# A paced list of transfers: turned weights ahead of loads and outputs, and a read-back of two transfers in place of four

## The chip, the core and the metric

The kernel runs on one core of a Trainium2 chip. The metric is the device time of one execution in microseconds, and lower is better. The kernel before took 1454.44 us, the median of three runs (1446.7 to 1459.63).

## What is computed

The reference has two parts: an attention with a threshold, and a bilinear feed-forward layer over its output. All numbers are 32-bit floats.

```python
# q, k, v: 8 batches x 8 heads x 576 rows x 64;  tau = 0.02
scores = scale * np.matmul(q, k.transpose(0, 1, 3, 2))
thresh = np.max(scores, axis=-1, keepdims=True) - tau
scores = np.where(scores >= thresh, scores, -1000000000.0)
scores = scores - np.max(scores, axis=-1, keepdims=True)
attn = np.exp(scores)
attn = attn / (np.sum(attn, axis=-1, keepdims=True) + 1e-09)
x = np.matmul(attn, v)      # then (B,H,S,D) -> (B*S, H*D): 4608 x 512
out = ((x @ w_a) * (x @ w_b)) @ w_out      # w_a, w_b: 512 x 1536;  w_out: 1536 x 512
```

## The kernel before

**Attention.** Two heads of a batch make a pair; there are 32 pairs. A pair has four units of 128 rows (u = 0 to 3) and one of the last 64 rows (u = 4). The outer loop (L974) takes one unit per slot. In slot g, PE makes the scores of unit g (`scores`, L379), DVE takes their maxima (L386), ACT the exponentials (L407), DVE masks and sums them (L410), and ACT divides by the sum (L429). The result `tw` lies with rows on the partitions, while the product with v needs it turned, with keys on the partitions.

**How the weights are turned.** For the first units PE turns them. From then on it is done in three steps that follow each other through the slots:

- slot g, `turn_blocks` of unit g-1: DVE turns blocks of 32 x 32 in place (L473), and four transfers of 144 KB (72 KB for u = 4) put them into DRAM (`swap<-tw`).
- slot g, `turn_back` of unit g-2: the unit is read back from DRAM into a tile `wT`, in transfers of 144 KB (`wT<-swap`), four for a unit of 128 rows, two for the last unit of a pair. There are two `wT` buffers (L441), and a product needs both.
- slot g, `weighted` of unit g-3: where that unit is the last of a half (u = 1 or u = 4), PE makes the product `pv` of the turned weights and v (L513), from which `xT`, the input of the feed-forward layer, is copied.

**Feed-forward.** Its matmuls (L673, L746, L803) are a generator, `ffn`, of which `advance` takes so many columns between the steps of the attention. The matmuls of both parts stand on PE in the order in which the program writes them; `keep_order` fixes that order on every engine, SP's queue included.

**The list of transfers.** All transfers of the main loop are issued by SP, in order. Up to slot 40 they are issued where they are posted (L142). From slot 41 on, `post` puts each entry, with its key and slot, at the end of a list, `bulk`. `passed` takes one entry off the front for every 320 columns (`PUMP`) of PE's work. `pump` issues its transfers and makes the first one wait for the last matmul written so far (L151 and the lines after it), so that transfers are spread along PE's work. `flush` takes entries off until those of a key are out: it is called where the program is about to use the data, in `prep` (Q and K), in `turn_back` (the stores of that unit) and in `weighted` (v and the read-backs). At the start of a slot, entries that were posted before the slot ahead of it are put out too (L977).

What is posted: `("tw", i, u)`, four entries of one transfer, in `turn_blocks`; `("wT", i, h)`, four entries of one transfer (two for u = 4), in `turn_back`; in `load`, `("k", i)`, four entries of one transfer, and `("q0", i)` and `("q1", i)`, two entries of two; `("v", i)`, two entries of two; `"out"`, one entry for each tile of results (`store`). Q and K are loaded three and four slots ahead of their first scores, and DVE turns them (`prep`, L347) one and two slots ahead of them.

Each transfer takes one of eight semaphores in turn, and SP waits for the transfer eight places earlier to have landed before it issues the next with the same semaphore.

Of the kernel before, what the change touches and what calls it, by code (L numbers as in the profile page):

```python
# [53 lines left out]
def kernel(  # L54
# [81 lines left out]
    bulk = []  # L136

    def post(key, *moves):

        if not state["paced"]:  # L140
            for move in moves:
                nc.sync.dma_start(*move)  # L142
        else:
            bulk.append((key, state["slot"], moves))

    def pump(count=1):

        for _ in range(min(count, len(bulk))):
            behind = next(x.name for x in reversed(nc.cur_bb.bb.instructions) if x.engine == mybir.EngineType.PE)
            for n, move in enumerate(bulk.pop(0)[2]):  # L150
                moved = nc.sync.dma_start(*move)  # L151
                if n == 0:
                    tc.add_manual_dep(
                        moved.ins, behind,
                        mybir.DependencyInfo(mybir.DependencyClass.Sync, mybir.DependencyReason.DATA),
                        reason="pace")

    def flush(*keys):

        while any(key in keys for key, _, _ in bulk):  # L160
            pump()

    def passed(columns):

        running["pump"] = running["pump"] + columns if bulk else 0
        while running["pump"] >= PUMP:
            running["pump"] -= PUMP
            pump()

    def load(i, name):  # L170

        b, hp = pairs[i]
        src = {"q": q, "k": k}[name[0]]
        n0, n1 = {"k": (0, NB), "q0": (0, HALF // Q), "q1": (HALF // Q, NB)}[name]
        bufs = HP if name == "k" else Q_BUFS
        most = NB if name == "k" else NB - HALF // Q
        t = work.tile([P, most, Q], FP32, tag=name[0] + "T", bufs=bufs, name=name[0] + "T")[:, 0:n1 - n0]
        for j in range(2):
            rows = src[b, 2 * hp + j].rearrange("(e n) d -> e n d" if name == "k" else "(n e) d -> e n d", e=Q)
            moves = [(t[(2 * j + h) * Q:(2 * j + h + 1) * Q], rows[:, n0:n1, h * Q:(h + 1) * Q]) for h in range(2)]  # L180
            for some in ([moves] if name != "k" else [moves[0:1], moves[1:2]]):
                post((name, i), *some)
        loaded.setdefault(i, {})[name] = t
# [9 lines left out]
    def load_v(i, again=False):  # L193
        b, hp = pairs[i]
        if not again:
            loaded[i]["v"] = loads.tile([P, NSLOT, D], FP32, tag="vm", bufs=HP, name="vm")
        for j in range(2):
            rows, half = v[b, 2 * hp + j], loaded[i]["v"][j * D:(j + 1) * D]
            if i >= HP or again:
                if i < HP:  # L200
                    rows = rows.rearrange("(c s p) d -> p c s d", c=2, p=Q)
                else:
                    rows = rows.rearrange("(p c s) d -> p c s d", c=2, p=Q)
                post(("v", i), *((half[c * Q:(c + 1) * Q], rows[:, c]) for c in range(2)))
            else:
                nc.sync.dma_start(half, rows.rearrange("(s p) d -> p s d", p=D))
# [21 lines left out]
    for F in range(NF):  # L228
# [3 lines left out]
    state = {"loaded": 0, "added": 0, "converted": 0, "rows": 0, "sums": False, "through": 0, "over": False,  # L232
             "layer": False, "paced": False, "slot": 0, "reading": False, "first": 0}
# [104 lines left out]
    prepared, scored, weights, turned, whole = {}, {}, {}, {}, {}  # L338
# [4 lines left out]
    def prep(i, name):  # L343

        flush((name, i))
        mT = loaded[i].pop(name).rearrange("p n e -> p (n e)")
        nc.vector.transpose(mT, mT)  # L347
        prepared.setdefault(i, {})[name] = mT
# [91 lines left out]
    def turned_tile():  # L440
        return work.tile([P, G + 1, NSLOT, Q], FP32, tag="wT", bufs=2, name="wT")  # L441
# [17 lines left out]
    def part(i, u):  # L459

        if i < HP:
            return {1: (i, 0), 3: (i, 1), NT: (i, 2)}.get(u)
        return {1: (i, 0), NT: (i, 1)}.get(u)
# [4 lines left out]
    def turn_blocks(i, u):  # L468

        ws, _ = weights.pop((i, u))  # L470
        t = whole.pop((i, u))
        for w in ws:
            nc.vector.transpose(w, w)  # L473
        if u < NT:
            swap = scratch.tile([G, P, NSLOT * Q], FP32, tag="swap", name="swap")
        else:
            swap = scratch.tile([2, P, NSLOT * Q], FP32, tag="swapt", name="swap")
        swaps[i, u] = swap
        for g in range(G):
            if u < NT:  # L480
                to, n = swap[g], G
            else:
                to, n = swap[g % 2, (1 - g // 2) * D:(2 - g // 2) * D], 2
            post(("tw", i, u), (to.rearrange("(r p) e -> p r e", p=Q),
                                t[g * Q:(g + 1) * Q, 0:n * NSLOT].rearrange("p (r s) e -> p r (s e)", r=n)))

    def turn_back(i, u):

        flush(("tw", i, u))
        swap = swaps.pop((i, u)).rearrange("g p e -> p g e")  # L490
        key = "wT", i, min(u // 2, 1) if i >= HP else u // 2
        if u < NT or i < HP:
            turned[i, u] = turned_tile()
            n = G if u < NT else 2
            for y in range(0, n, 1):
                post(key, (turned[i, u][:, y:y + 1].rearrange("p g s e -> p g (s e)"), swap[:, y:y + 1]))
        else:
            for y in range(2):
                post(key, (turned[i, 2 + y][:, G].rearrange("p s e -> p (s e)"), swap[:, y]))
# [76 lines left out]
    def weighted(i, h):  # L576

        b, hp = pairs[i]
        flush(("v", i), ("wT", i, h))
        n = width(i, h)  # L580
        if h < 2:
            groups = G + (n > HALF)
            wT = [turned.pop((i, 2 * h + y))[:, 0:groups] for y in range(2)]
        else:
            t = turned.pop((i, NT))
            wT = [t[:, y:y + 1] for y in range(2)]
        pv = product([lambda rows, s, t=t: t[rows, :, s] for t in wT], loaded[i]["v"], n)
        read = [], []
        if h < 2:
            if hp == 0:  # L590
                x_of[b, h] = x_tile("xT")
            settle(x_of[b, h][:, hp, :], pv, 0, P, read)
            settled[b, h] = hp + 1
            if hp == HP - 1:
                del settled[b, h]
                complete.append((x_of.pop((b, h)), ("half", b, h)))
        if n % HALF:
            t = b % GT
            if hp == 0 and t == 0:
                xtail_of[b // GT] = x_tile("xt")  # L600
            settle(xtail_of[b // GT][:, hp, t * TAIL:(t + 1) * TAIL], pv, (n - TAIL) // 2, n // 2, read)
            del loaded[i], prepared[i]
            if hp == HP - 1 and t == GT - 1:
                complete.append((xtail_of.pop(b // GT), ("tail", b - t, 0)))
# [364 lines left out]
    n = 0  # L969
# [4 lines left out]
    for g in range(len(units) + PV_LAG):  # L974
        written = len(pending)
        state["slot"], state["paced"] = g, g > 40
        while bulk and bulk[0][1] < g - 1:  # L977
            pump()
# [4 lines left out]
        if BY_PE + 1 < g <= len(units) + 1:  # L983
            n = g - PV_LAG
            back = (1 if BY_PE <= n and part(*units[n]) else 0,)
            if not back[0]:
                turn_back(*units[g - 2])
        if here:
            i, u = units[g]
# [40 lines left out]
        if g > BY_PE:  # L1030
            n = g - PV_LAG
            held = 0.0
            if BY_PE <= n < len(units) and part(*units[n]):
                held = 384 - (PORTIONS[2] + PORTIONS[3]) * pace + NSLOT * width(*part(*units[n])) // 2
                held = min(max(held, 0.0), 384)
            advance(PORTIONS[1] * pace - held)
            if BY_PE <= n < len(units) and part(*units[n]):
                p, h = part(*units[n])
                if pairs[p][1] == 0:
                    make_x(2 if h == 1 and p >= HP and pairs[p][0] % GT == 0 else 1)  # L1040
                make_room()
                weighted(*part(*units[n]))
                passed(NSLOT * width(*part(*units[n])) // 2)
                running["owed"] -= NSLOT * width(*part(*units[n])) // 2
            if back and back[0] > 0:
                turn_back(*units[g - 2])
# [85 lines left out]
```

## Time and profile before

| What | Value |
|---|---|
| Median of three runs | 1454.44 us (1446.7 to 1459.63) |
| The profiled execution | 1455.69 us, its span 1453.8 us |
| TensorE clock granted, mean of the span | 0.991 |
| Transfers that SP issues | 1736, of which `wT<-swap` 544 and `swap<-tw` 608 |
| Bytes moved | 223.32 MB, 154 GB/s over the span |
| `wT<-swap`: issue, and from issue to landing (medians) | 383 ns (paced), 3.1 us |
| `swap<-tw`: from issue to landing (median, 144 KB) | 2.9 us |

The page gives busy time by engine, then the span in 40 slices, the DMA queues, the chain of work that ended last, the groups of instructions with the idle time of their engine ahead of them, and the DMA issues. PE is TensorE's matmuls, PEld its weight loads; each matmul of 32-bit floats stands as two records. SPq is SP's own queue: its instructions only issue transfers. In a row of groups the part after the bar is busy time, mean duration in ns, and the idle time of the engine just before, with what ended most of it. A row of waits reads: who waited, for whom, us in total, times, the longest. A row of stretches reads: from:to, length, then busy us and instructions of PE, PEld, DVE, ACT and POOL, the granted clock, the share of the DMA engines, GB/s. A row of the timeline reads: start, us, engine, line, operation, how many merged.

### The profile page before, as it was taken

The numbers are of one execution on the slowest core, as the hardware profiler recorded it, in microseconds if no ns is written. First come the engines' busy times: TensorE is split into PE (matmuls) and PEld (weight loads), VectorE is DVE, ScalarE is ACT, GpSimd is POOL, SyncE is SP. The second block draws the span as 40 slices with busy tenths as digits, with TensorE's granted clock in tenths as the row PEclk, the third lists the DMA queues.
The fourth block names the chain that finished last, engine by engine and source line by source line (L and its number), as shares of the span: only waits on it lengthen the run. The fifth ranks groups of instructions, "written<-read, shape, count | busy, mean of one in ns | idle before, by whom it ended". The sixth has DMA issues, their size and how long they took to land.

```text
span 1453.8 us, 77671 instructions
## 1 busy us (share of the span) xinstructions
PE 1388.9 (96%) x34208; PEld 1255.0 (86%) x34208; DVE 1017.0 (70%) x2244; ACT 684.2 (47%) x1244; POOL 480.6 (33%) x668
## 2 busy tenths in 40 slices
PE   6889999998999989999999999999999999999998
PEld 4777897987979889999999899898888879998896
DVE  6898677787767867677757686778757677755223
ACT  5787454544545445545444445344535445430110
POOL 2664803423060605132333333241506060605000
PEclk8899999999999999999999999999999999999999
DMA  9976667666756776567545676466655676450000
GB/s 203 240 217 184 157 168 200 178 162 171 190 154 152 170 188 158 151 161 191 158 121 140 159 187 191 120 158 160 190 148 138 161 184 195 122 152 28 4 18 17
DMA packets 330914, 223.32 MB, mean 154 GB/s; under 512 B 175441, under 2 KB 314705, under 8 KB 330577
## 3 DMA queue, kind: packets, MB, share of 16 engines
q1 hardware_dynamic: 328064, 217.76, 58.7%
q8 instruction: 270, 4.42, 1.3%
q10 hardware_dynamic: 2512, 0.59, 0.2%
q14 instruction: 68, 0.55, 0.1%
HBM read 128.58 MB, written 89.65 MB: 150 GB/s over the span
## 4 chain that ended last, share of the span: by engine, by line
PE 86%; DMA 5%; DVE 3%; issue 2%; SPq 2%; ACT 1%; DVEq 0%; ACTq 0%
PE pab L673 26%; PE po L803 20%; PE pab L746 18%; PE pv L513 10%; PE sc L379 10%; DMA wT<-swap 3%; PE po L849 1%; SPq L142 1%; DMA vm<-in_v_dram 1%; DMA sums_u<-in_q_dram 1%; PE tp L454 1%; DVE mx L386 1%; DVE tw L473 1%; DVE tw L410 1%; DMA sums_u<-in_k_dram 0%
## 5 line engine op out<-in xcount | busy, mean ns | idle before, releaser
L386 DVE TENSOR_REDUCE mx<-sc 128x1 f32<-128x576 f32 x288 | 206.2, 752 | 138.0 <-PE sc L379 126.7
L429 ACT ACTIVATE tw<-tw,rcp 128x576 f32<-128x576 f32 x272 | 197.8, 769 | 220.6 <-DVE rcp L423 220.6
L407 ACT ACTIVATE tw<-sc,bias,scalars 128x576 f32<-128x576 f32 x288 | 239.3, 831 | 10.1 <-ACT bias L406 0.4
L639 POOL TENSOR_TENSOR h<-h,u 128x512 f32<-128x512 f32 x28 | 35.1, 1273 | 613.8 <-DVE h L716 469.4
L803 PE MATMUL po<-wo_sb,h 64*64 64x256 f32 x3264 | 230.2, 377 | 0.0
L410 DVE SCALAR_TENSOR_TENSOR tw<-sc,thr,tw 128x576 f32<-128x576 f32 x288 | 222.9, 798 | 9.0 <-ACT tw L407 7.2
L513 PE MATMUL pv<-wT,vm 64*64 64x160 f32 (+3 forms) x5184 | 188.3, 278 | 25.7 <-DMA wT<-swap 19.3
L513 PEld LDWEIGHTS pv<-wT,vm 64*64 64x64 f32 x5184 | 169.7, 136 | 40.2 <-issue 15.1
L379 PE MATMUL sc<-kT,qT 64*64 64x288 f32 x2016 | 196.9, 404 | 3.2 <-issue 2.0
L473 DVE STREAM_TRANSPOSE tw<-tw 128x576 f32<-128x576 f32 x272 | 196.1, 754 | 0.8 <-ACT tw L429 0.8
L803 PEld LDWEIGHTS po<-wo_sb,h 64*64 64x64 f32 x3264 | 168.0, 133 | 26.7
L803 PE MATMUL po<-sums_u,h 64*64 64x256 f32 x2448 | 169.3, 376 | 0.3 <-DVE h L754 0.3
L772 POOL TENSOR_TENSOR h<-h 128x256 f32<-128x256 f32 x168 | 117.4, 730 | 124.4 <-PE po L803 120.7
L379 PEld LDWEIGHTS sc<-kT,qT 64*64 64x64 f32 x2016 | 117.9, 133 | 28.5 <-issue 5.7
L803 PEld LDWEIGHTS po<-sums_u,h 64*64 64x64 f32 x2448 | 123.0, 133 | 21.6 <-DVE h L754 1.2
L673 PE MATMUL pab<-xU,wb_sb 64*64 64x128 f32 x4096 | 137.1, 270 | 0.0
L673 PEld LDWEIGHTS pab<-xU,wb_sb 64*64 64x64 f32 x4096 | 130.0, 133 | 2.0
L406 ACT ACTIVATE bias<-mx,scalars 128x1 f32<-128x1 f32 x288 | 83.2, 289 | 88.7 <-DVE mx L386 88.5
L521 DVE COPY xT<-pv 64x128 f32<-64x128 f32 (+1 forms) x136 | 38.2, 281 | 120.1 <-PE pv L513 118.9
L520 ACT COPY xT<-pv 128x128 f32<-128x128 f32 (+1 forms) x68 | 17.6, 259 | 215.5 <-PE pv L513 215.3
L673 PE MATMUL pab<-xS,wa_sb 64*64 64x128 f32 x2048 | 112.2, 269 | 0.0
L746 PE MATMUL pab<-xS,wb_sb 64*64 64x256 f32 (+1 forms) x1536 | 101.3, 359 | 0.9 <-issue 0.9
(138 smaller groups left out, 2473.3 us busy)
## 6 DMA issues: line engine op xcount, KB each, us to landing
wT<-swap SPq DMA_DIRECT2D x544, 144.0 KB, 3.1
swap<-tw SPq DMA_DIRECT2D x480, 144.0 KB, 2.9
vm<-in_v_dram SPq DMA_DIRECT2D x128, 72.0 KB, 2.4
swap<-tw SPq DMA_DIRECT2D x128, 72.0 KB, 3.0
kT<-in_k_dram SPq DMA_DIRECT2D x112, 72.0 KB, 3.1
out_dram<-kept SPq DMA_DIRECT2D x30, 256.0 KB, 3.0
qT<-in_q_dram SPq DMA_DIRECT2D x112, 40.0 KB, 2.3
qT<-in_q_dram SPq DMA_DIRECT2D x112, 32.0 KB, 2.8
```

The source lines that it names most:

```text
L379: nc.tensor.matmul(sc[j if u < NT else 0][to, c], qT[r, q0:q0 + D], kT[r, c * SH:(c + 1) * SH], start=True, stop=True)
L386: nc.vector.tensor_reduce(mx[:, c], sc[j], axis=AX.XY, op=ALU.max)
L406: nc.scalar.activation(bias[:, j:j + 1], mx[:, j:j + 1], AF.Copy, scale=e_nscale)
L407: nc.scalar.activation(wb[j], sb[j], AF.Exp, bias=bias[:, j:j + 1], scale=e_scale)
L410: nc.vector.scalar_tensor_tensor(out=wv, in0=sb[j], scalar=thr[:, j:j + 1], in1=wv, op0=ALU.is_ge, op1=ALU.mult, accum_out=sums[:, j:j + 1])
L429: nc.scalar.activation(w, w, AF.Copy, scale=rcp[:, j:j + 1])
L473: nc.vector.transpose(w, w)
L513: nc.tensor.matmul(pv[c * D:(c + 1) * D, y], vm[rows, s], wT[y](rows, s), start=(s == 0), stop=(s == NSLOT - 1))
L673: nc.tensor.matmul(out[c * D:(c + 1) * D, r, f * P:(f + 1) * P], w[g][k][rows, w0:w0 + D], moving[k][rows], start=(fresh and k == 0 and f ...
L746: nc.tensor.matmul(pab[c * D:(c + 1) * D, r], w[rows, f // n, k, fs + c * D:fs + (c + 1) * D], moving, start=(k == 0), stop=(k == H - 1))
L772: (nc.vector if state["over"] else nc.gpsimd).tensor_tensor(*a, **kw)
L803: nc.tensor.matmul(po[c * D:(c + 1) * D, r, y], ht[rows, t0:t0 + D], other[rows, f], start=(f == 0), stop=(f == NF // 2 - 1))
```

## The change

It has three parts, all in the list and in what is posted to it.

1. `post` no longer puts every entry at the end. An entry of turned weights (key `tw` or `wT`) goes ahead of those at the end of the list that are neither, as long as these were posted in the present slot or the one before it. Entries of turned weights keep their order among themselves.
2. `flush` issues what it takes off the list without the wait for the last matmul.
3. A unit's read-back is posted in two entries, each a transfer of 288 KB that covers two of the four groups, in place of four of 144 KB. The last unit of a later pair (the `else` branch) keeps its two of 144 KB.

```diff
         else:
-            bulk.append((key, state["slot"], moves))
-
-    def pump(count=1):
+            at = len(bulk)
+            if key[0] in ("tw", "wT"):
+                while at and bulk[at - 1][0][0] not in ("tw", "wT") and bulk[at - 1][1] >= state["slot"] - 1:
+                    at -= 1
+            bulk.insert(at, (key, state["slot"], moves))
+
+    def pump(count=1, paced=True):
...
                 moved = nc.sync.dma_start(*move)
-                if n == 0:
+                if n == 0 and paced:
                     tc.add_manual_dep(
...
         while any(key in keys for key, _, _ in bulk):
-            pump()
+            pump(1, False)
...
             n = G if u < NT else 2
-            for y in range(0, n, 1):
-                post(key, (turned[i, u][:, y:y + 1].rearrange("p g s e -> p g (s e)"), swap[:, y:y + 1]))
+            for y in range(0, n, 2):
+                post(key, (turned[i, u][:, y:y + 2].rearrange("p g s e -> p g (s e)"), swap[:, y:y + 2]))
```

## The prediction

> **What bounds it now.** I read the busy shares first, then what PE waits for, then the stretch around one such wait in SP's own order.
>
> ```profile
> PE 1388.9 (96%) x34208; PEld 1255.0 (86%) x34208; DVE 1017.0 (70%) x2244; ACT 684.2 (47%) x1244; POOL 480.6 (33%) x668
> L513 PE MATMUL pv<-wT,vm 64*64 64x160 f32 (+3 forms) x5184 | 188.3, 278 | 25.7 <-DMA wT<-swap 19.3
> ```
>
> PE is busy for 96% of the span, so nothing that leaves its matmuls alone can give more than its idle time. The group with the largest part of that idle time is the product of turned weights and v, and it waits for the read-back `wT<-swap`. Asking the same for the stage in which the list is paced (335 to 1320 us):
>
> ```profile
> 335.00:1320.00 985.00, 961.98 (x24309) 883.21 (x24313) 699.71 (x1556) 466.91 (x834) 312.37 (x470) 1.00 0.62 160
> PE pv L513 <- DMA wT<-swap: 15.9, 9, 3.6
> PE pv L513 <- issue: 1.5, 2, 1.3
> ```
>
> 985.0 - 962.0 = 23.0 us of PE idle in this stage, 15.9 of it in nine waits for a read-back. DVE has 285 us idle there, DMA is 62% busy: neither is the bound. Why the read-backs are late, at the wait of 2.38 us before the product at 530 us (SP's queue, then PE):
>
> ```profile
> 519.17 3.22 SPq L151 DMA_DIRECT2D swap<-tw  x4
> 522.49 1.90 SPq L151 DMA_DIRECT2D wT<-swap  x4
> 524.49 0.37 SPq L151 DMA_DIRECT2D out_dram<-kept  x1
> 524.95 3.24 SPq L151 DMA_DIRECT2D wT<-swap  x4
> 528.30 3.98 SPq L151 DMA_DIRECT2D swap<-tw  x4
> 533.01 3.60 PE L513 MATMUL pv<-wT,vm 64*64 64x128 f32 x67 [2.38 <-DMA wT<-swap]
> 533.40:536.80 3.40, 3.40 (x73) 3.40 (x68) 0.00 (x0) 0.00 (x0) 0.00 (x0) 0.50 0.70 134
> ```
>
> SP issues without a pause, one transfer in about 0.48 us (1.90/4), with a longer one now and then. The last read-back of this product is paced behind a matmul that ended at 521.2, is issued at 527.8 and lands at 532.7. Its lateness is SP's queue (6.6 us), not the transfer (4.9 us from issue to landing, 3.1 is the median). The last line is a second cost: after the wait TensorE ran 3.4 us at half clock.
>
> **What the Trainium skill says.** "Perfetto Trace Analysis", section on the life of an HWDGE DMA instruction: the profiled time of a DMA instruction is the sequencer's generation of descriptors, not the movement. The trace agrees: 0.38 us per issue, 3.1 us to landing. Same page, "What 'DMA-bound' means": an issuing track that is solid with slices is bound in descriptor generation; so SP is here in bursts. "TensorE: Matmul & The Clock Gate", part 1: after about 3.4 us without enough work TensorE falls to half clock. Here the clock halves for 3.4 us twice in this stage, after the waits of 3.6 and 2.4 us.
>
> **The change, part by part.** The list's order is fixed by the program, so I counted for both versions behind which matmul each transfer is put out, and put PE's times of this trace to those matmuls. PE's, ACT's, DVE's and POOL's own orders don't change; only SP's does.
>
> *Read-backs ahead of loads and outputs.* For the 48 products whose read-backs are paced, the last one is put out 9.8 us (mean; 5.6 at least) ahead of the product now and 11.8 us (10.0 at least) with the change. The one at 530 gains 2.6 us: two entries for each unit in place of four, and no output between them. Now nine of the 48 land after PE is ready, together 14.6 us late (the trace's waits: 15.9 less the 3.6 of the next part, 12.3, and 1.5 of "issue"). Shifting each by its own gain leaves none late; the smallest reserves are 0.3 to 0.4 us (three products). Gain 12.3 + 1.5 = 13.8 us.
>
> *Half as many issues.* 544 read-back issues become 300: 244 fewer, at 0.48 us 117 us of SP's time, hidden except where SP is the last to be waited for. One is the 3.6 us wait at 334 us: SP issues without pause from 316 us, and eight read-backs on that way become four, 4 x 0.48 = 1.9 us. Before 335 us two more waits stand (19.3 - 15.9 = 3.4 us, of 1.5 and 1.9): four and two issues fewer there give 1.9 and 0.9. Together 4.7 us. The issue of a 288 KB transfer is not in the trace: at least today's 0.38 us, at most 0.77 (two of today's). K loads, with 576 runs of 128 bytes for a transfer, take 0.58; so I take 0.5. At the upper end the 4.7 us go. Landing: "DMA: Bandwidth & Descriptors", anatomy of one DMA, gives a fixed 2.0 us and bytes/436 GB/s, so 0.34 us more than for 144 KB, an estimate by that page; the trace's 3.1 against the page's 2.3 for 144 KB says that it is low under load. The 256 KB outputs take 3.0 to landing. I take 0.4 us (0 to 1). It uses up the three smallest reserves, so I charge 1.5 us (0 to 5).
>
> *Clock.* Two half-clock stretches of 3.4 us cost 1.7 us each. The one after 530 goes with its wait; the other, after 334, I count half. 2.6 us.
>
> *Loads fall back.* This is the price. A K load is now put out 2.2 us later in the median of 21, Q loads are unchanged in the median, some up to 3.5 later. Who waits is DVE, with the transpose at L347, and behind it on DVE stand the masks (L410) and maxima (L386) that free PSUM banks. Now there is one wait:
>
> ```profile
>   DMA kT<-in_k_dram: 0.3, 1
> ```
>
> Between landing and transpose there are 3.7 us for K, 4.0 and 5.6 for the two kinds of Q (medians), 0.2 at the least. Shifted by their own changes, 5 of 67 come late, together 8.5 us on DVE. DVE is 71% busy in this stage and itself waits for PE often, so I charge PE a third, 3 us (0 to 20, see the last rival). V loads keep 28 us or more, outputs move by 3.5 us at most: nothing.
>
> *Stores of turned tiles ahead too.* They come earlier, so SP reaches the first one of a unit before DVE has turned it: in 120 of 120 units by PE's clock, 70 now; the sum of these distances goes from 142 to 252 us. SP's present lag hides much of it. A waiting SP holds all that is behind; this is already charged in part, since "SPq L151 <- DVE tw L473" is 80.8 us today. It offsets the 117 us of SP's time saved, so I give the loads no relief from fewer issues. The reverse exists too: 23 read-backs are put out less than 3.5 us behind their own store today, 2 with the change, so SP will stand less often for a store's landing.
>
> *Flush without pace.* 29 entries are forced out so today (28 stores, one read-back); with the new order none is. It costs and gains nothing of itself.
>
> Sum: 13.8 + 4.7 + 2.6 - 1.5 - 3.0 = 16.6 us. The profiled execution took 1455.7 us (span 1453.8), 1.3 above the median 1454.4; from the median, 1454.4 - 16.6 = **1438 us**.
>
> **Rivals.**
> 1. *As summed* (0.60): 1438, own range 1430 to 1445. The floor is all idle of the stage, 23.0, with 3.4 before it and 3.4 of clock: 1425.
> 2. *Half hidden* (0.30): read-backs are earlier in the list, but SP stands for DVE's transposes in front of them and two 288 KB transfers take as long as four; half of the 13.8 stays, 4.7 goes. 13.8/2 + 1.3 - 3 = 5 us: 1449. For it: the distances of 252 us. Against: the store ahead of a read-back is put out 2.7 us or more before it. That the change does not do what it says belongs here: if 288 KB issue as two, only the order is left.
> 3. *Loads become the wait* (0.10): if K and Q loads come 3 us later than their place says, because SP stands for DVE ahead of them, 27 of 67 are late by 60 us together on DVE. Some two thirds of that, 40 us, would reach PE through the banks, less the 21 won: about +19, 1473 us. It decides from about 2 us of such lateness (21 loads, 35 us on DVE, 23 on PE). For it: K's 3.7 us of reserve shrink to 1.5. Against: the distance to DVE is 2.0 us in the median unit (4.3 at most), and the list is emptied sooner.
>
> A measurement of this kernel can tell about 1%, 14.5 us, from no change (its three runs spread over 13). Faster by over 1% is below 1439.9: just over four fifths of case 1 and a little of 2, 0.52. Slower, above 1469: 0.08. Within: 0.40. Range for 8 in 10: 1428 (case 1 with the loads free and most small idle gone) to 1452 (most of case 2).
>
> **What would show it.** Right: `wT<-swap` x300 at 144 and 288 KB; the wait of `pv` for it in the paced stage under 4 us; PE's idle time there down from 23 to some 10; no half-clock stretch near 530. Wrong in the loads: L347 waits for `kT` or `qT` of over 10 us in sum, with PE's `sc` or `pab` waiting for DVE. Wrong in the issue: read-back issues of 0.7 us or more, and SP still solid around 530. The prediction fails if PE's idle time stays near 23 us, or moves from `pv` to `sc`.

## The result, and the profile after

The changed kernel takes 1448.78 us (median of 21 runs, 1442.15 to 1452.1) against 1456.26 us before (21 runs, 1446.7 to 1463.98). The ratio is 0.9941 with a 95% interval of 0.9927 to 0.9955: it is faster by 0.6%, where 1.1% was forecast. Half of the forecast gain is missing, and the question is where it went. The profiled executions show 1444.2 us after and 1453.8 us before (spans), with clocks of 0.997 and 0.991; their difference of 9.6 us is what the traces can explain.

The page of the changed kernel, busy shares, one row of groups, two rows of DMA issues (out<-in, count, KB each, us to landing):

```profile
PE 1383.9 (96%) x34208; PEld 1265.5 (88%) x34208; DVE 1015.8 (70%) x2244; ACT 684.7 (47%) x1244; POOL 480.6 (33%) x668
...
L517 PE MATMUL pv<-wT,vm 64*64 64x160 f32 (+3 forms) x5184 | 179.8, 272 | 6.8 <-issue 3.5
...
wT<-swap SPq DMA_DIRECT2D x244, 288.0 KB, 4.2
...
wT<-swap SPq DMA_DIRECT2D x56, 144.0 KB, 2.7
```

The product's idle time fell from 25.7 to 6.8 us, and its wait for the read-back has left the row. A transfer of 288 KB is one issue, and lands 4.2 us after it. The stage of the paced list, as a stretch, and then what PE waited for in it (who, for whom, us, times, longest):

```profile
335.00:1320.00 985.00, 968.29 (x24482) 887.90 (x24484) 710.19 (x1571) 469.44 (x838) 321.14 (x483) 1.00 0.61 160
```

```profile
PE pab L677 <- issue: 5.5, 8, 1.5
PE sc L383 <- issue: 2.4, 7, 0.5
PE pv L517 <- issue: 1.6, 2, 1.3
PE pv L517 <- DMA swap<-tw: 1.5, 1, 1.5
PE pv L517 <- PE pab L750: 1.0, 2, 0.5
PE pab L750 <- issue: 0.9, 1, 0.9
```

PE's idle time here is 985.0 - 968.3 = 16.7 us, from 23.0. Of the 15.9 us of waits for a read-back none is left by name; the 1.5 us put to `swap<-tw` stand at 335 us, at the product that waited 3.58 us before. Yet the idle time fell by only 6.3 us. What took the place is "issue", time in which PE waited for nothing that the profile shows: 5.5 + 2.4 + 1.6 + 0.9 = 10.4 us, from 4.0. The half-clock stretches at 338.8 and 533.4 us are gone; there is one of 3.4 us at 241.4 us, ahead of the stage. DVE's waits for its loads, as the answer for L351 lists them, and SP's largest wait:

```profile
  DMA kT<-in_k_dram: 8.0, 7
  DMA qT<-in_q_dram: 2.1, 2
```

```profile
SPq L155 <- DVE tw L477: 148.3, 72, 6.5
```

Loads came late nine times, and SP now stands 148.3 us for DVE's turned tiles (80.8 before).

Setting the same matmul of both traces against each other gives the gain along the way: -1.0 us at 325 us, +6.2 at 550 to 600, +2.4 at 825, +11.3 at 1200, +9.2 at the end. It is won in steps of 1 to 4 us at single products (4.1 at 334 us, of which the wait itself gives 2.0, from 3.58 to 1.54 us; 3.9 at 530) and lost again between them.

### The profile page after: what moved, and what is told of

It is laid out like the page before. It is cut to its first block, busy times and chain, and to the rows that moved or that the text cites. A ratio compares the mean times of both kernels' runs of the same rounds, so it can differ in the third digit from the quotient of the medians.

```text
span 1444.2 us, 77110 instructions
## 1 busy us (share of the span) xinstructions
PE 1383.9 (96%) x34208; PEld 1265.5 (88%) x34208; DVE 1015.8 (70%) x2244; ACT 684.7 (47%) x1244; POOL 480.6 (33%) x668
## 4 chain that ended last, share of the span: by engine, by line
PE 87%; DVE 5%; DMA 4%; issue 2%; SPq 1%; ACT 1%; DVEq 0%; ACTq 0%
PE pab L677 26%; PE po L807 20%; PE pab L750 19%; PE sc L383 10%; PE pv L517 9%; PE po L853 1%; DMA kT<-in_k_dram 1%; DVE mx L390 1%; DMA sums_u<-in_k_dram 1%; DVE tw L414 1%; DVE tw L477 1%; DMA raw<-in_moe_w_a_dram 1%; DMA raw<-in_moe_w_b_dram 0%; DVE thr L391 0%; DVE low L298 0%
## 5 line engine op out<-in xcount | busy, mean ns | idle before, releaser
L807 PEld LDWEIGHTS po<-wo_sb,h 64*64 64x64 f32 x3264 | 175.5, 133 | 19.4
L517 PE MATMUL pv<-wT,vm 64*64 64x160 f32 (+3 forms) x5184 | 179.8, 272 | 6.8 <-issue 3.5
L517 PEld LDWEIGHTS pv<-wT,vm 64*64 64x64 f32 x5184 | 166.2, 133 | 16.3 <-issue 7.6
L807 PEld LDWEIGHTS po<-sums_u,h 64*64 64x64 f32 x2448 | 129.7, 133 | 16.3 <-DVE h L758 1.4
L524 ACT COPY xT<-pv 128x128 f32<-128x128 f32 (+1 forms) x68 | 17.7, 260 | 193.0 <-PE pv L517 193.0
```

The costliest lines, as they stand in the source:

```text
L517: nc.tensor.matmul(pv[c * D:(c + 1) * D, y], vm[rows, s], wT[y](rows, s), start=(s == 0), stop=(s == NSLOT - 1))
L807: nc.tensor.matmul(po[c * D:(c + 1) * D, r, y], ht[rows, t0:t0 + D], other[rows, f], start=(f == 0), stop=(f == NF // 2 - 1))
```

## The experiments

The runs came in four sets. The kernels of a set ran on one chip, beside the kernel before, and each ratio is to the kernel before of the same set. The first and third set ran on one chip, the second and fourth on another. In the texts of what was expected, a "dry run" of PE is a gap in which PE has run out of instructions; what that rests on follows below.

**First set: which part brings the gain?** `reorder4` is the changed kernel with its new order, but four transfers of 144 KB:

```diff
-            for y in range(0, n, 2):
-                post(key, (turned[i, u][:, y:y + 2].rearrange("p g s e -> p g (s e)"), swap[:, y:y + 2]))
+            for y in range(0, n, 1):
+                post(key, (turned[i, u][:, y:y + 1].rearrange("p g s e -> p g (s e)"), swap[:, y:y + 1]))
```

> The new order alone, with four read-backs of 144 KB. By place in the list the last read-back is put out 10.7 us ahead of its product (before 9.8, changed kernel 11.7) and K loads 4.5 us (median) ahead of DVE (8.1 and 5.4). Theory A (the 288 KB transfers hold back PE's own instruction fetches): PE runs dry at most 3 times in the paced stage (changed kernel 9 times, 7 us), read-back waits are mostly gone, K loads are late for 12 to 20 us; ratio to before 0.990 to 0.996. Theory B (the order bunches transfers and so holds back the fetches): PE runs dry 7 times or more; ratio 0.994 to 1.000. Theory C (when PE runs dry is chance): no relation to either part.

`halves` is the kernel before with its old list, and only the third part of the change:

```diff
-            for y in range(0, n, 1):
-                post(key, (turned[i, u][:, y:y + 1].rearrange("p g s e -> p g (s e)"), swap[:, y:y + 1]))
+            for y in range(0, n, 2):
+                post(key, (turned[i, u][:, y:y + 2].rearrange("p g s e -> p g (s e)"), swap[:, y:y + 2]))
```

> Two read-backs of 288 KB in the old order. By place the last read-back is put out 11.0 us ahead of its product, 7.8 at least (before 9.8 and 5.6), and K and Q loads earlier than before too (8.6 and 11.8 us in the median). Theory A: 6 to 12 dry runs of PE in the paced stage, so the ratio is 0.993 to 0.998 although most read-back waits are gone. Theory B: at most 3 dry runs, no late loads, ratio 0.987 to 0.992, so that this part alone beats both kernels. The prediction's own view, that the order brings most of the gain: read-back waits of 6 us or more stay, ratio 0.996 or more.

`kkeep` is the changed kernel, but turned weights don't pass K loads; `again_after` is one more execution of the changed kernel.

```diff
-                while at and bulk[at - 1][0][0] not in ("tw", "wT") and bulk[at - 1][1] >= state["slot"] - 1:
+                while at and bulk[at - 1][0][0] not in ("tw", "wT", "k") and bulk[at - 1][1] >= state["slot"] - 1:
```

> The changed kernel, but K loads are not passed over (Q, v and outputs still are). By place K loads are back at 8.6 us ahead of DVE, read-backs stay at 11.3 us. If late loads are what the gain was lost to: waits of the transpose for K fall from 8.0 us to under 1 us and the ratio to before from 0.994 to 0.990 or less. If it is PE's instruction fetches: same number of dry runs (7 to 11) and a ratio of 0.992 to 0.995.

> The changed kernel once more, for a second trace. If PE's dry runs follow from the order of transfers, they stand again at 7 to 11 in the paced stage and mostly at the same places in PE's work; if they are chance, their number falls toward that of before (1) or their places differ.

`halves` measured 0.9899 (0.9867 to 0.9931), `kkeep` 0.9914 (0.9882 to 0.9947), and `reorder4` 1.0013 (0.9996 to 1.003). The order alone gives nothing; the halves alone give all that the change gives. `halves` lies inside the range of theory B, although its trace has the eight dry runs of theory A, so the ratio alone does not part the two. `kkeep` lies between its two cases: no K load is late any more, but Q loads are, by 8.0 us, and the dry runs stay (11). `again_after` has 11 again, six of them in the same blocks of instructions. PE's waits in `reorder4`, and what DVE's transposes (L351) waited for there:

```profile
PE pv L517 <- DMA wT<-swap: 5.2, 1, 5.2
PE sc L383 <- DVE h L699: 5.1, 2, 3.1
PE sc L383 <- issue: 4.7, 7, 1.9
PE sc L383 <- DVE xt L525: 3.1, 2, 2.5
```

```profile
  DMA qT<-in_q_dram: 24.2, 15
  DMA kT<-in_k_dram: 24.0, 14
```

The order does move the read-backs' waits away (15.9 to 5.2 us), but it moves them to the loads: 29 of them are late by 48 us, DVE stands before them, and the scores wait for DVE. This is the third rival, with its mechanism and much of its size on DVE (27 loads and 60 us were worked out), on the variant that keeps 144 KB; but its time is that of before, not 19 us more. With the halves, in their old order, both waits are gone. The stage as a stretch, and PE's waits:

```profile
335.00:1320.00 985.00, 973.39 (x24572) 886.45 (x24568) 713.50 (x1581) 473.65 (x847) 323.74 (x487) 1.00 0.62 161
```

```profile
PE sc L379 <- issue: 2.3, 6, 0.5
PE pv L513 <- issue: 2.2, 4, 1.1
PE pab L673 <- issue: 1.8, 4, 0.7
PE pv L513 <- DVE kept L503: 1.5, 1, 1.5
PE pv L513 <- DMA wT<-swap: 1.1, 2, 0.6
```

985.0 - 973.4 = 11.6 us of idle time is the lowest of all runs. No load is late.

**Second set: the place in the list, or SP's time?** With two entries in place of four the read-backs also stand earlier in the paced list (11.0 us ahead of the product by the times of before, in place of 9.8). `halves_paced` takes that away: an empty entry ahead of each keeps the place and the pace of before, and SP only has 244 issues fewer.

```diff
             for y in range(0, n, 2):
+                post(key)
                 post(key, (turned[i, u][:, y:y + 2].rearrange("p g s e -> p g (s e)"), swap[:, y:y + 2]))
```

> Old order, two read-backs of 288 KB, but an empty entry in the list ahead of each, so that the last one stands at its place of before (9.8 us ahead of the product in the mean, 5.6 at least) and loads too. If the gain of the halves comes from SP's issues alone: ratio to before 0.989 to 0.993, read-back waits under 6 us in the paced stage. If it comes from the earlier place in the list: waits of 8 us or more stay and the ratio is 0.995 to 1.000.

`one576` goes further in the same direction, one transfer of 576 KB for a unit in the old order; `wt_ahead` is the changed kernel with stores left in their place, so that only read-backs pass the loads; `again_before` is one more execution of the kernel before.

```diff
-            for y in range(0, n, 1):
-                post(key, (turned[i, u][:, y:y + 1].rearrange("p g s e -> p g (s e)"), swap[:, y:y + 1]))
+            for y in range(0, n, n):
+                post(key, (turned[i, u][:, y:y + n].rearrange("p g s e -> p g (s e)"), swap[:, y:y + n]))
```

> Old order, one read-back of 576 KB for a unit. By place 11.6 us ahead of the product, loads earlier again (K 9.3 us in the median). If entries and issues are what counts: ratio 0.985 to 0.989. If larger transfers hold back PE's instruction fetches: 10 or more dry runs of PE in the paced stage, fetches later than with 288 KB, and a ratio of 0.990 to 0.996.

```diff
-            if key[0] in ("tw", "wT"):
+            if key[0] == "wT":
```

> The changed kernel, but only read-backs pass loads and outputs; stores of turned tiles stay in line. By place read-backs stand as in the changed kernel (11.7 us), K loads at 7.6 us (changed kernel 5.4, before 8.1). If it is the early stores, at which SP stands for DVE, that cost: SP's waits for DVE's turned tiles fall from 148 us to about 90, waits of DVE for loads from 10 us to under 2 us, ratio 0.988 to 0.991. If any passing of loads costs: DVE waits 5 us or more for loads, ratio 0.992 to 0.996.

> The kernel before once more, for a second trace. Read-back waits of 15 us or more in the paced stage and at most 4 dry runs of PE; if dry runs are chance, 7 or more may stand here too.

`halves_paced` measured 0.9869 (0.9825 to 0.9912). PE's wait for read-backs in its stage:

```profile
PE pv L514 <- DMA wT<-swap: 4.0, 4, 1.4
```

In the old places, with the old pace, that is 4.0 us in place of 15.9, and no load is late. So the place in the list is not needed: it was SP's time that made the read-backs late, and the fewer issues that end it. A read-back's issue takes 0.38 to 0.41 us (medians), at 144, 288 and 576 KB alike. `wt_ahead` measured 0.9902 (0.9866 to 0.9938), and can't be told from `halves_paced`; its waits (SP for DVE's tiles 122.3 us, DVE for loads 7.3) are neither of the two cases expected.

`one576` was the surprise: 1.0006 (0.9982 to 1.003), slower than either case expected, although it issues least. Its stretch, PE's waits and its read-backs:

```profile
335.00:1320.00 985.00, 957.59 (x24204) 859.45 (x24200) 699.53 (x1556) 470.61 (x836) 309.80 (x463) 1.00 0.62 160
```

```profile
PE pab L673 <- issue: 15.3, 15, 2.2
PE sc L379 <- issue: 3.7, 8, 0.8
PE pv L513 <- issue: 2.9, 3, 1.5
PE pv L513 <- DVE kept L503: 1.5, 1, 1.5
PE pab L746 <- issue: 1.1, 3, 0.4
```

```profile
wT<-swap SPq DMA_DIRECT2D x120, 576.0 KB, 5.1
```

No wait for a read-back and none for a load is left, and still PE is idle for 27.4 us: 23.0 of it is "issue". This is the same kind of time that took the place of the waits in the changed kernel.

**What the "issue" time is.** The matmuls around the longest such gap of the changed kernel (start, us, engine, line, operation, how many merged):

```profile
811.26 0.86 PE L677 MATMUL pab<-xU,more_u 64*64 64x128 f32 x18
813.62 0.27 PE L677 MATMUL pab<-xU,more_u 64*64 64x128 f32 x1 [1.50 <-issue]
```

PE stops in the middle of a group of matmuls of one kind, and the profile shows nothing that it waits for. The trace also has a queue, `q8 instruction`, with 269 packets of 16 KB, one for every 256 instructions of PE's queue, 1.0 us each in the median (0.9 to 2.1). Its packets around the gap, and around the one of 2.20 us in `one576`:

```
changed kernel  packets 800.32-801.46, 804.87-806.01, 811.22-812.19, 814.94-816.18   PE idle 812.12-813.62
one576          packets 530.98-531.91, 536.74-537.87, 540.42-541.38                  PE idle 537.07-539.27
```

The packet comes late: in the changed kernel 6.35 us after the one before it, while the three blocks of 256 instructions ahead of the gap took 3.7 to 4.0 us each (5.0 in the median of the stage). PE resumes 1.4 us after it has ended, both times. I counted the gaps of over 0.1 us in which PE and its weight loads wait for nothing visible, that stand at the same place of a block (192 instructions past a multiple of 256), and that end 0.9 to 1.8 us after such a packet: 11 in the stage of the changed kernel, 7.4 us in all; 2 of 1.0 us before; 25 of 19.9 us in `one576`, beside 23.0 us of "issue" in all. I call them dry gaps. As I picked them by place and packet, the count is a description; the last set tests the place. Nor does their number part 144 KB from 288: `again_before` has 7 of 3.5 us, the number that was named as a sign of chance, and `reorder4` 6 of 3.0 us, between its theories.

The lateness can also be read from all packets of the stage (188 to 193), whether PE waits or not. In the median a packet starts 0.7 to 1.1 us after PE has begun the instruction 192 past a multiple of 256. Those that start more than 2 us after it number 7, 16 and 13 in the three traces with read-backs of 144 KB, 22 to 34 in the twelve with 288 KB (30 in `halves_paced`, at the old pace), and 43 and 49 in the two with 576 KB. So the packets do come later with larger read-backs, apart from any choice of gaps.

The Trainium skill, "Runtime: NRT & Kernel Launch", section "Instruction fetch mechanics", describes such a refill: blocks of 16 KiB or 256 instructions through the sequencer's own DMA queue, its cost mostly hidden. The trace agrees on the blocks, and for most of them on the cost: in the stage of the changed kernel 11 gaps stand against 193 packets, in `one576` 25 against 190.

**Third set: bytes or runs?** If large read-backs delay the packets, is it by their bytes, or by their many short runs (1152 bytes)? The tile in DRAM laid row by row makes runs of 2304 bytes in `halves_rows` and of 4608 bytes in `one576_rows`. `halves_b` and `after_b` repeat the two kernels on one chip.

```diff
-            swap = scratch.tile([G, P, NSLOT * Q], FP32, tag="swap", name="swap")
+            swap = scratch.tile([P, G, NSLOT * Q], FP32, tag="swap", name="swap")
...
-                to, n = swap[g], G
+                to, n = swap[:, g], G
...
-        swap = swaps.pop((i, u)).rearrange("g p e -> p g e")
+        swap = swaps.pop((i, u))
```

> Halves in the old order, and the turned tile laid out in DRAM row by row, so that a read-back of 288 KB has 128 runs of 2304 bytes in place of 256 of 1152. If it is the bytes ahead of PE's instruction fetches that make PE run dry: dry runs as with the halves (8 and 3.4 us in its profile), ratio to before 0.986 to 0.992. If it is the number of packets: at most 4 dry runs and a ratio of 0.983 to 0.988.

> One read-back of 576 KB for a unit in the old order, in 128 runs of 4608 bytes in place of 512 of 1152. Bytes: 20 dry runs or more, 15 us or more, ratio 0.997 to 1.003 as with short runs. Packets: dry runs fall to 10 or fewer, and the ratio to 0.985 to 0.991.

> The halves in the old order once more, beside the changed kernel on one chip. If the new order costs: ratio 0.988 to 0.992, below that of the changed kernel by 0.003 to 0.006, dry runs 5 to 10. If the two are the same and the first reading was chance: both 0.992 to 0.995.

> The changed kernel on the same chip as halves_b. Ratio 0.993 to 0.996, 9 to 13 dry runs in the paced stage, 8 us or more of DVE waiting for K and Q loads. The rival says no difference from halves_b in time.

`halves_rows` measured 0.9873 (0.9853 to 0.9892), `one576_rows` 1.0046 (1.0027 to 1.0066), with 22.5 us dry: longer runs do not end the dry gaps. Of the two it is the bytes of a transfer that count, not its runs. `halves_b` measured 0.9901 (0.988 to 0.9922) and `after_b` 0.9896 (0.9876 to 0.9916): here the changed kernel and the halves alone are the same, as the rival has it, and the changed kernel is better than the 0.993 to 0.996 expected of it.

**Fourth set: does the place move with the instructions?** `shifted` is the changed kernel in which 36 transposes of the start are made twice, 72 PE instructions more ahead of the stage. If the gaps belong to certain matmuls they stay; if they belong to the blocks they move. `after_c` and `rows_b` repeat `after` and `halves_rows`.

```diff
-        for c in range(2):
+        for c in (0, 1, 0, 1) if i else (0, 1):
```

> The changed kernel a third time, since its ratio was 0.994 on record and 0.990 beside the halves. If the shortfall on record was of that set of runs: 0.988 to 0.992 again, PE idle in the paced stage 15 to 18 us. If it is steady and the second reading was chance: 0.993 to 0.996.

> Halves with the turned tile laid out row by row once more, beside the changed kernel. If it is the better kernel: a ratio of 0.985 to 0.989, at least 0.002 below that of the changed kernel. The rival says that the two can't be told apart.

> The changed kernel with 36 transposes of the start made twice, so that the boundaries of PE's instruction fetches lie 72 instructions earlier in all later work. If PE runs dry where a fetch meets a burst of transfers: the dry runs stand again at the same point of the fetch (192 instructions past a multiple of 256) but mostly at other places in PE's work than in the other traces of this kernel, and their sum may be anything from 2 to 12 us. If they come from places in the program: they stay where they were, at another point of the fetch.

In `shifted` there are 16 gaps of 7.3 us, again 192 past a multiple of 256, so at other matmuls than before. The place was not put there by the choice: of all 20 gaps in its stage for which the profile shows no cause, 16 stand there, and the largest of the others, 1.3 us before the product at 1186 us, shows what a fixed place in the program does. It stands 17 past a multiple of 256 in the four other traces of the changed kernel, and 89 past it here, 72 further. Of the 16 gaps, eight are in blocks in which one of those four traces has one too (55, 56, 115, 124, 145, 189, 190, 205), three in a block next to one, and five in new ones (61, 72, 122, 151, 196). So the place follows the block's bounds; that the transfers of the moment decide which block is hit is likely, but not shown. `after_c` measured 0.9935 (0.9911 to 0.9959), `rows_b` 0.9904 (0.987 to 0.9937); the two can't be told apart.

All runs, with the stage from 335 to 1320 us of one profile each (dry gaps from 330 us on):

| Kernel | Ratio, 95% interval | PE idle, us | for read-backs | "issue" | of that, dry | DVE for K and Q |
|---|---|---|---|---|---|---|
| before | 1 | 23.0 | 15.9 | 4.0 | 1.0 | 0.3 |
| again_before | one execution | 23.5 | 12.6 | 6.9 | 3.5 | 1.1 |
| reorder4 | 1.0013, 0.9996-1.003 | 26.3 | 5.2 | 9.0 | 3.0 | 48.2 |
| after, 21 runs | 0.9941, 0.9927-0.9955 | 16.7 | 0 | 10.4 | 7.4 | 10.1 |
| again_after | one execution | 17.9 | 0 | 10.4 | 8.4 | 10.7 |
| after_b | 0.9896, 0.9876-0.9916 | 13.6 | 0 | 8.7 | 5.2 | 9.0 |
| after_c | 0.9935, 0.9911-0.9959 | 19.2 | 0 | 12.1 | 9.3 | 18.8 |
| shifted | one execution | 17.7 | 0.3 | 11.1 | 7.3 | 9.3 |
| kkeep | 0.9914, 0.9882-0.9947 | 16.4 | 1.2 | 11.3 | 8.1 | 8.0 |
| wt_ahead | 0.9902, 0.9866-0.9938 | 20.8 | 2.7 | 13.5 | 10.0 | 7.3 |
| halves | 0.9899, 0.9867-0.9931 | 11.6 | 1.1 | 7.1 | 3.4 | 0 |
| halves_b | 0.9901, 0.988-0.9922 | 14.4 | 1.0 | 9.3 | 6.2 | 0 |
| halves_paced | 0.9869, 0.9825-0.9912 | 17.0 | 4.0 | 9.0 | 5.8 | 0 |
| halves_rows | 0.9873, 0.9853-0.9892 | 17.8 | 1.4 | 12.5 | 9.7 | 0 |
| rows_b | 0.9904, 0.987-0.9937 | 16.8 | 0.4 | 12.3 | 8.9 | 0 |
| one576 | 1.0006, 0.9982-1.003 | 27.4 | 0 | 23.0 | 19.9 | 0 |
| one576_rows | 1.0046, 1.0027-1.0066 | 30.1 | 0 | 25.6 | 22.5 | 0 |

The column "issue" needs no choice of mine, and tells the same as the dry gaps: 4 to 9 us with read-backs of 144 KB, 7 to 14 with 288, 23 to 26 with 576. The first two ranges touch. One profile of a kernel differs from another of the same kernel by up to 5.6 us of idle time, so single rows can't be ranked by less.

## Why the prediction was half right

The mechanism that bounds the stage was read rightly: SP's queue makes the read-backs late, the products wait for them, and the change ends that. The time measured, 1448.78 us, lies in the range; between the medians the gain is 1456.26 - 1448.78 = 7.5 us in place of 16.6. Two steps failed: the sum counted 1.5 us of "issue" time as gained and put nothing for instructions that reach PE late, and there 6.4 us were lost; and it gave the gain at the read-backs to the order, where the fewer issues bring it. By its steps:

- **"Read-backs ahead of loads and outputs", 13.8 us: the effect is there, its cause is wrong.** The waits went, as worked out (12.3 us), but the 1.5 us of "issue" in the term stayed (1.6 after): 1.3 of it is the gap at the fixed product near 1186 us, which is no late read-back. And `reorder4`, which has the order and not the halves, wins nothing, and `halves_paced`, which has none of the earlier places, has as good a ratio as any. The places by matmul that I shifted told where a transfer *may* be issued; when it is issued was set by what SP still had to issue ahead of it, and of that I kept the old lag. At 530 us the reading was one-sided too: the last read-back landed 4.9 us after its issue, 1.8 more than the median, and the whole wait was 2.4 us. The gain that I gave to the order belongs to the next term.
- **"Half as many issues", 4.7 us: the wrongly sized term.** I counted 244 fewer issues as hidden except at three waits, and gave back the rest as "no relief". The 244 x 0.48 us = 117 us taken from SP, which is solid in bursts, carry the whole gain. The 334 us wait fell by 2.0 us (1.9 worked out). Of the 2.8 us before 335 nothing was left in this profile: the wait at 240 us went (the lead rose from 2.3 to 4.4 us), but the scores waited 2.09 us at 239 us for DVE, with the half clock behind it, and with two gaps of 0.8 and 1.0 us more the sum at 325 us is -1.0 us.
- **Issue and landing.** The issue takes 0.38 to 0.41 us (0.5 taken). The landing rose by 1.1 us, from 3.1 to 4.2 (0.4 taken; the Trainium skill, "DMA: Bandwidth & Descriptors", section "Anatomy of one DMA", gives an estimate of 0.34 by a formula for transfers that GpSimd issues, while these are SP's; the measurement decides). No product pays for it in this profile: the charge of 1.5 us was not needed.
- **Clock, 2.6 us.** Both stretches in the stage went, 2 x 1.7 = 3.4 us. The new one at 241 us costs 1.7 of it again.
- **"Loads fall back", 3.0 us.** Nine waits of 10.1 us on DVE, where five of 8.5 us were worked out; PE's idle time ahead of the scores rose by 1.5 us. Right in kind and near in size. But the term exists only because of the order: with `halves` no load is late.
- **Stores ahead** make SP stand longer for DVE, as said: 80.8 to 148.3 us. It is not a cost of the new order alone, as `halves` has 131.0 us of it too.
- **The step that is missing.** No term stands for PE's own instructions, which come by DMA as well. Their dry gaps took 7.4 us in the stage of this profile, against 1.0 before. The stage was to give 13.8 + 1.9 + 2.6 - 1.5 - 3.0 = 13.8 us. Its accounts show 14.4 us of waits for read-backs gone (14.2 worked out) and 3.4 us of clock won (2.6), 1.7 us lost at the loads and the smaller waits (3.0, and 1.5 for the landing), and 6.4 us lost in "issue" time, where 1.5 were to be won. That makes 9.7 us; matmul against matmul it is 10.2 (9.2 + 1.0). The miss in the stage is thus the "issue" time, 7.9 us, made up in part by the other terms. The other 3.8 us (2.8 and 1.0) are those before the stage.

*Rivals.* The second (half hidden, 1449 us) has the measured time by luck, not by its mechanism: no read-back wait was left. The third (loads) is what `reorder4` shows. In the changed kernel the fewer issues keep it away.

*What stays open.* The changed kernel was 0.9941 and 0.9935 in two sets, and 0.9896 in a third, where the intervals of the first and the last do not overlap. In that set the gain is 1460.21 - 1443.86 = 16.4 us, the size that was forecast, although its profile has dry gaps too; had that been the first measurement, the sum would have come out right by luck. Its profile has less of two things (5.2 us dry against 7.4 and 9.3; loads 9.0 against 10.1 and 18.8 us), but it is one execution each, and these differences do not add up to 9 us. The last two values come from different chips. What makes a set differ was not found, so how much of the missing gain between the medians is PE's instructions stays open; the accounts above hold for the pair of profiles.

Nor is it settled whether the new order costs anything beside the halves: they were equal where both ran on one chip.

That larger read-backs come with later packets is measured at three sizes; that they stand ahead of the packets in the DMA engines' own queues is argued, as no view shows a packet waiting. Nor was load in bursts ruled out as a cause: `halves_paced` keeps the old pace at 288 KB, but no run does at 576. Between 50 and 115 us, where weights are loaded by 256 and 512 KB and DMA's share is 0.88, the kernel before itself has seven such gaps of 8.4 us. That the gaps are what cancels the gain at 576 KB is read from the profiles of two kernels, where little else is left; no run takes the gaps away.

No version was shown to beat the changed kernel: `halves_rows` is not clear of it in the same set, and `halves_paced` was not run beside it.

## What to carry to other kernels

Where one queue issues everything in order and is solid ahead of a wait, count its issues first: fewer, larger transfers ended the wait here at the old place in the order, while moving one kind of transfer ahead of another only moved the wait. But the size had an optimum, with 288 KB better than 144 and 576: after enlarging transfers, look at PE's "issue" time, and at whether its gaps stand at a fixed place of 256 instructions. When two changes come together, run each alone before giving either the gain.

## What the runs showed of the hardware

- PE ran out of instructions in a straight-line program: its blocks of 16 KB arrived later with read-backs of 288 KB (3.4 to 10.0 us of gaps in the stage) and of 576 KB (19.9 and 22.5 us) than with 144 KB (1.0 to 3.5 us), at the same mean DMA load of 60 to 63%. What differs is the size of one read-back and, with it, their number and the bytes put out at once. The Trainium skill, "DMA: Bandwidth & Descriptors", section "Bandwidth", advises batches of 1 MiB and more for the sake of bandwidth; here, where DMA was not the bound, 576 KB lost all that 288 KB won.
- The issue time of a read-back on SP did not depend on its size: 0.38 to 0.41 us at 144, 288 and 576 KB. The landing did: 3.1, 4.2 and 5.1 us (medians).
- SP's long issues fall together with PE's packets: in the stage of the kernel before, 128 of the 130 issues of over 1 us start within 0.6 us of the start of one. For example, issues of 1.2 to 1.8 us start at 500.86, 505.65, 510.40, 515.24 and 519.63 us, and packets at 500.92, 505.47, 510.27, 515.38 and 519.64 us.
- The clock halved for 3.4 us after waits of 2.1 us (241 us, after) and 2.2 us (540 us, `one576`), the second of them a dry gap, so such a gap can cost its length and 1.7 us more. Not every wait of that length does: 2.5 us at 358 us before was followed by none.
